# Issuing each 64 KB-row load of a decode attention kernel as two interleaved half transfers, one on SP's queue and one on ACT's

## The chip, the core and the metric

One core of one Trainium2 chip runs the whole program. The metric is device time in microseconds (us) of one execution, as the median of several runs. A profiled execution gives, besides its own time, a trace of every instruction and of every DMA queue.

## What is computed

A decode step (one token for each of two batch rows) of a transformer block with adaptive layer norm. Cut to what matters:

```python
mod = (silu(c) @ w_mod).reshape(2, 6, 1, 512)          # sa, ca, ga, sb, cb, gb
h = layernorm(x) * (1 + ca) + sa
q = (h @ wq) as 32 heads of 128
p = softmax(q . k_cache / sqrt(128))                   # 2 batches, 32 heads, 4096 keys
x = x + ga * ((p @ v_cache) @ wo)
h = layernorm(x) * (1 + cb) + sb
x = x + gb * (mish(h @ w1 + b1) @ w2)
```

All of it is float32. The two caches are 2 x 32 x 4096 x 128 each, so the work on one head begins with 4 MB of keys and 4 MB of values that are read once and never again. The weights come on top: 297 MB are read in all.

## The kernel before

**The stream.** Everything large comes from HBM as a stream of 36 loads, numbered 0 to 35, laid out beforehand in `stream` (line 31) so that a load is one array with 128 rows, one for each SBUF partition. Load 0 is two transfers with rows of 32 KB: the first holds the weights m01 (shift and scale of the first norm), wq0 and wq1, the second the keys k0 of head 0. Loads 1 to 31 are one transfer each, with rows of 64 KB (`ROW` = 16384 floats, 8 MB in all; sizes here are in units of 1024): the keys of head n and, in what room is left, halves of values, a wq or a wo. Loads 32 to 35 are twelve smaller transfers: one with rows of 56 KB for load 32, two of 32 KB for load 33, three for load 34 and six for load 35.

**The rooms.** `load` (line 134) takes one of three buffers, "room", of 64 KB per partition in turn and issues the load's transfers by `nc.sync.dma_start` (line 141), that is, on the queue of SP. `used` (line 146) keeps account: when every key of load n-3 has been used, load n is issued into the same room. It is called once at the start, which issues loads 0, 1 and 2 at once (line 156), and then after each step that finishes with a part of a room. No scheduler moves anything: the instructions of each engine stand in the order in which the Python code issues them, and each waits by semaphores for what it needs.

**The start.** On ACT's queue the kernel issues two small transfers: `cx` (line 161: 8 rows of 1 KB, the conditioning vector c and the token x) and `bias` (line 164: 128 rows of 48 bytes). From `cx` come the silu of c (`cps`, `sg`, `ct`) and the first layer norm (`mean_a`, `var_a`, `rs_a`, `xn`). With m01 in room 0, `modulation` (line 240) gives `modps`; from it come `hq`, `hps`, `hcw` (lines 270 to 280), and `project_q` (line 286) multiplies by wq0 and wq1; ACT scales the product into `q0` and `q1` (line 292).

**One head.** VectorE (DVE) does the scores: `products` (line 318) multiplies the keys in the room by q, in place, and `sums` (line 321) adds up over the 128 elements. `row_max` (lines 326 to 330) and `soft_max` (line 334 on DVE, line 337 on ACT) give the exponentials `e`, TensorE multiplies them by the values in `weighted_v` (line 359), and every four heads `value_sums`, `head_values` and `project_o` (lines 374, 382, 385, 390) bring the result through wo. The loop over the 32 heads issues `products(h)`, `soft_max(h-1)`, any `project_q`, `sums(h)`, then `used(("k", h))` (line 446), then the values whose load has come with these keys, then `row_max(h)`. So load h+3 is as a rule issued behind `sums(h)` in the code, or a little later, behind the last matmul on the values of that room.

**The end.** After head 31 come the rest of the values, the second norm, the two dense layers (`w1ps` line 514, `yps` line 556) and the store of 32 rows (line 566).

Of the kernel before, what the change touches and what calls it, by code (L numbers as in the profile page):

```python
# [13 lines left out]
P = 128  # L14
# [13 lines left out]
ROW = 2 * BIG  # L28
# [41 lines left out]
def kernel(  # L70
# [15 lines left out]
    nc = tc.nc  # L86
# [29 lines left out]
    def take(t, keys):  # L116
        lo = 0
        for key in keys:
            kind, n = key[:2]
            part = t[:, lo : lo + SIZES[kind]]  # L120
            lo += SIZES[kind]
            if kind == "k":
                k_t[n] = part.rearrange("p (j d) -> p j d", d=DH)
            elif kind == "v":
                v_t[n, key[2]] = part.rearrange("p (c n) -> p c n", n=512)
            elif kind in ("wq", "wo"):
                (wq_t if kind == "wq" else wo_t)[n] = part.rearrange("p (k n) -> p k n", k=G)
            else:
                w_t[kind] = part.rearrange("p (k n) -> p k n", k=NCH if kind == "w2" else G)
# [4 lines left out]
    def load(n):  # L134

        t = kvp.tile([P, ROW], F32, tag="room", name=f"room{n}", bufs=3)
        lo = 0
        for keys, srcs in loads[n]:
            take(t[:, lo:], keys)
            for src in srcs:  # L140
                nc.sync.dma_start(out=t[:, lo : lo + src.shape[-1]], in_=src)  # L141
                lo += src.shape[-1]

    loaded = 0
# [1 line left out]
    def used(*keys):  # L146

        nonlocal loaded
        done.update(keys)
        while loaded < len(loads) and (  # L150
            loaded < 3 or all(key in done for keys, _ in loads[loaded - 3] for key in keys)
        ):
            load(loaded)
            loaded += 1
# [16 lines left out]
        out=fold, in_=ident.rearrange("p (g r) -> p r g", g=G), axis=AX.X, op=ALU.add  # L171
# [3 lines left out]
        out=mean_w, in0=fold[:, None, :].to_broadcast([P, G, R]), scalar1=1.0 / D, scalar2=None, op0=ALU.mult  # L175
# [4 lines left out]
        out=half, in_=ident.rearrange("p (b r) -> p r b", b=B), axis=AX.X, op=ALU.add  # L180
# [330 lines left out]
    for k in range(G):  # L511
        lo = 0
# [9 lines left out]
    lo = 0  # L522
    for g in reversed(range(G)):
# [3 lines left out]
        lo = hi  # L527
# [112 lines left out]
```

## Time and profile before

| | us |
|---|---|
| median of 3 runs | 698.69 (698.48 to 698.77) |
| the profiled execution, its own time | 698.42 |
| its span, first to last instruction | 696.6 |
| DVE busy in the span | 587.7 (84%) |
| PE (matmul) busy | 283.8 (41%) |
| ACT busy | 44.0 (6%) |

The page of the profile gives the span in 40 slices of 17.4 us, with the busy share of each engine in tenths, the mean busy share of the 16 DMA engines and the GB/s that they moved. The queue of SP appears in the DMA list as q1, that of ACT as q10. "L318 DVE" is an instruction of line 318 on DVE. The view of DMA issues gives for each line the size and the median time from issue to landing. The chain of waits goes back from the last instruction to what released it.

### The profile page before, as it was taken

How to read it: one execution, taken by the hardware profiler on the slowest of the kernel's cores; microseconds unless marked ns; L12 is line 12 of the kernel's file. 1: busy time of each engine (PE TensorE's matmuls, PEld its weight loads, DVE VectorE, ACT ScalarE, POOL GpSimd, SP SyncE). 2: the span in 40 equal slices, each digit the busy share in tenths (PEclk: the TensorE clock that was granted, in tenths of full speed). 3: DMA queues.
4: the chain of work that ended last, by engine and by line, in shares of the span. 5: the costliest groups of instructions: out<-in, count | busy, mean ns of one | idle time of the engine just before them, and what ended most of it. 6: DMA issues, size and time to landing. Idle time of an engine off the chain costs nothing.

```text
span 696.6 us, 3912 instructions
## 1 busy us (share of the span) xinstructions
PE 283.8 (41%) x1636; PEld 102.4 (15%) x1636; DVE 587.7 (84%) x220; ACT 44.0 (6%) x168; POOL 4.2 (1%) x19
## 2 busy tenths in 40 slices
PE   3403334335245615335232806234333526224686
PEld 1200001001011201102100301011101101001234
DVE  3799899999999999999999999999999999899002
ACT  1000000000000000000000000000000000000010
POOL 2000000000000000000000000000000000000000
PEclk9855666667566665656585756666575657555789
DMA  9999999999999999999999999999999999999996
GB/s 392 452 421 421 426 474 421 419 429 421 467 422 425 429 425 456 429 425 426 433 448 429 426 429 437 440 430 429 433 437 437 429 425 422 452 427 420 423 422 270
DMA packets 6706, 297.49 MB, mean 427 GB/s; under 512 B 888, under 2 KB 928, under 8 KB 1184
## 3 DMA queue, kind: packets, MB, share of 16 engines
q1 hardware_dynamic: 6528, 297.23, 98.9%
q8 instruction: 13, 0.21, 0.1%
q10 hardware_dynamic: 160, 0.01, 0.0%
q14 instruction: 5, 0.04, 0.0%
HBM read 297.22 MB, written 0.02 MB: 427 GB/s over the span
## 4 chain that ended last, share of the span: by engine, by line
DMA 69%; DVE 28%; PE 2%; issue 0%; SPq 0%; ACT 0%; DVEq 0%
DMA room<-in_load 69%; DVE room L318 14%; DVE s L321 14%; PE ov L359 1%; PE qps L291 1%; PE modps L247 1%; PE yps L556 0%; SPq L141 0%; DVE m L334 0%; DVE hcw L280 0%; ACT q L292 0%; PE hps L237 0%; DVE y L564 0%; DVE hq L270 0%; DVE hq L271 0%
## 5 line engine op out<-in xcount | busy, mean ns | idle before, releaser
L318 DVE TENSOR_TENSOR room<-room,q 128x8192 f32<-128x8192 f32 x32 | 278.2, 8692 | 46.8 <-DMA room<-in_load 42.4
L321 DVE TENSOR_REDUCE s<-room 128x64 f32<-128x8192 f32 x32 | 277.9, 8683 | 0.4 <-DVE m L334 0.3
L359 PE MATMUL ov<-room,e 128*32 128x512 f32 x1024 | 176.4, 842 | 80.1 <-ACT e L337 63.9
L330 PE MATMUL mt<-d,same 128*128 128x64 f32 x64 | 18.2, 378 | 195.8 <-DVE d L328 195.8
L359 PEld LDWEIGHTS ov<-room,e 128*32 128x32 f32 x1024 | 39.2, 145 | 188.6 <-issue 133.8
L337 ACT ACTIVATE e<-s,m 64x64 f32<-64x64 f32 x64 | 22.1, 345 | 556.6 <-DVE m L334 555.8
L330 PEld LDWEIGHTS mt<-d,same 128*128 128x128 f32 x64 | 13.1, 254 | 225.8 <-DVE d L328 179.3
L291 PE MATMUL qps<-room,hcw 128*128 128x512 f32 x64 | 43.4, 844 | 4.8 <-DMA room<-in_load 4.0
L345 PE MATMUL l<-l,ones 128*128 128x8 f32 x16 | 4.6, 358 | 75.1 <-ACT e L337 75.1
L382 PE MATMUL otp<-pick,o 128*128 128x8 f32 (+2 forms) x72 | 13.4, 313 | 33.9 <-ACT o L374 32.0
L291 PEld LDWEIGHTS qps<-room,hcw 128*128 128x128 f32 x64 | 16.8, 274 | 26.4 <-issue 20.5
L374 DVE COPY o<-ov 128x256 f32<-128x256 f32 x1 | 0.4, 425 | 22.6 <-ACT o L374 22.6
L382 PEld LDWEIGHTS otp<-pick,o 128*128 128x128 f32 x72 | 12.6, 263 | 42.3 <-ACT o L374 39.4
L345 PEld LDWEIGHTS l<-l,ones 128*128 128x128 f32 x16 | 3.8, 296 | 76.5 <-ACT e L337 76.5
L334 DVE TENSOR_REDUCE m<-mt 128x1 f32<-128x64 f32 x32 | 6.9, 217 | 7.6 <-PE mt L330 7.6
L390 PE MATMUL att<-room,ot 128*32 128x512 f32 x62 | 10.1, 709 | 5.2 <-DMA room<-in_load 4.7
L337 ACT ACTIVATION_READ_ACCUMULATOR e<-s,m 64x1 f32 x64 | 11.8, 185 | 0.0
L328 DVE TENSOR_SCALAR d<-half,m 128x64 f32<-128x64 f32 x32 | 8.1, 254 | 1.1
L247 PE MATMUL modps<-room,ct 128*32 128x128 f32 (+1 forms) x160 | 8.1, 346 | 2.3 <-DMA room<-in_load 2.2
L326 DVE TENSOR_REDUCE m<-s 128x1 f32<-128x64 f32 x32 | 7.0, 217 | 0.9
L374 ACT COPY o<-ov 128x512 f32<-128x512 f32 (+1 forms) x9 | 5.0, 561 | 25.9 <-PE ov L359 25.7
L247 PEld LDWEIGHTS modps<-room,ct 128*32 128x32 f32 x160 | 5.0, 121 | 4.6 <-issue 4.4
(101 smaller groups left out, 60.6 us busy)
## 6 DMA issues: line engine op xcount, KB each, us to landing
room<-in_load SPq DMA_DIRECT2D x4, 4096.0 KB, 25.0
room<-in_load SPq DMA_DIRECT2D x1, 7168.0 KB, 39.1
room<-in_load SPq DMA_DIRECT2D x1, 3072.0 KB, 26.2
room<-in_load SPq DMA_DIRECT2D x3, 1024.0 KB, 28.3
room<-in_load SPq DMA_DIRECT2D x1, 2400.0 KB
room<-in_load SPq DMA_DIRECT2D x1, 2304.0 KB, 20.4
room<-in_load SPq DMA_DIRECT2D x1, 1376.0 KB, 15.8
room<-in_load SPq DMA_DIRECT2D x2, 256.0 KB, 22.8
```

The lines of the kernel that those rows point to most:

```text
L247: nc.tensor.matmul(ps[R * g : R * (g + 1)], lhsT=ct[:, k, :], rhs=t[:, k, :].rearrange("p (m n) -> p m n", m=n)[:, :, P * g : P * (g + 1)] ...
L291: nc.tensor.matmul(ps, lhsT=hcw[:, k, :], rhs=wq_t[ch][:, k, :], start=(k == 0), stop=(k == G - 1))
L318: nc.vector.tensor_tensor(out=k_t[h], in0=k_t[h], in1=qv, op=ALU.mult)
L321: nc.vector.tensor_reduce(out=s_t[h], in_=k_t[h], axis=AX.X, op=ALU.add)
L326: nc.vector.tensor_reduce(out=m_t[h][:, 0:1], in_=s_t[h], axis=AX.X, op=ALU.max)
L328: nc.vector.tensor_scalar(out=d, in0=half, scalar1=m_t[h][:, 0:1], scalar2=None, op0=ALU.mult)
L330: nc.tensor.matmul(mps[h], lhsT=same, rhs=d, start=True, stop=True)
L337: nc.scalar.activation(e_t[i][own_b, :, M * i + 4 * b : M * i + 4 * b + 4], s_t[h][own_b].rearrange("p (c m) -> p c m", m=4), AF.Exp, bias ...
L345: nc.tensor.matmul(lps[n], lhsT=ones, rhs=sum_t[n % 2], start=True, stop=True)
L359: nc.tensor.matmul(ov[bank][R * g : R * (g + 1), :], lhsT=e_t[h % HC][:, NB // 2 * part + c, :], rhs=v_t[h, part][:, c, :], start=(first a ...
L382: nc.tensor.matmul(tps[:, x], lhsT=o_t[m], rhs=pick_t[n][:, m, x], start=(m == 0), stop=(m == 3),)
L390: nc.tensor.matmul(att[R * i : R * (i + 1), :], lhsT=ot_t[n % 2][:, i, :], rhs=wo_t[n][:, i, :], start=(n == 0), stop=(n == H // HC - (2 i ...
```

## The change

The inner loop of `load` issues a transfer with rows of 64 KB as two: the rows of the even partitions by SP and those of the odd partitions by ACT, each 64 rows of 64 KB. All the other transfers stay one transfer on SP.

```diff
             for src in srcs:
-                nc.sync.dma_start(out=t[:, lo : lo + src.shape[-1]], in_=src)
+                queues = (nc.sync, nc.scalar) if src.shape[-1] == ROW else (nc.sync,)
+                for i, queue in enumerate(queues):
+                    rows = slice(i, P, len(queues))
+                    queue.dma_start(out=t[rows, lo : lo + src.shape[-1]], in_=src[rows])
                 lo += src.shape[-1]
```

It meets loads 1 to 31. In the program that comes of it SP has as many transfers as before, 31 of them with 64 rows in place of 128; ACT has 31 more. The odd halves of loads 1 and 2 stand first on ACT, ahead of `cx`, since line 156 comes before line 161. From load 3 on, ACT's half stands where `used` issues it: behind the exponentials of head n-4 and ahead of those of head n-3, and it waits for the same things as SP's half (the DVE and PE instructions that last read the room, and the transfers that last wrote it). Three lines are added, so line 318 of before is line 321 after, and so on.

## The prediction

> **What bounds the kernel now.** I read the page first: busy shares, then the DMA lines, then the chain that ended last.
>
> ```profile
> span 696.6 us, 3912 instructions
> PE 283.8 (41%) x1636; PEld 102.4 (15%) x1636; DVE 587.7 (84%) x220; ACT 44.0 (6%) x168; POOL 4.2 (1%) x19
> ...
> q1 hardware_dynamic: 6528, 297.23, 98.9%
> ...
> q10 hardware_dynamic: 160, 0.01, 0.0%
> ...
> DMA 69%; DVE 28%; PE 2%; issue 0%; SPq 0%; ACT 0%; DVEq 0%
> ```
>
> The packets of SP's queue (q1) fill 98.9% of the time of 16 engines. The chain's 28% on DVE looks like a second bound, so I looked at stretches of 100 us (the last two columns are DMA share and GB/s) and at DVE in order of time.
>
> ```profile
> 200.00:300.00 100.00, 44.69 (x208) 14.79 (x204) 93.11 (x28) 6.49 (x25) 0.00 (x0) 0.65 1.00 433
> 300.00:400.00 100.00, 39.70 (x192) 13.74 (x184) 93.06 (x28) 5.73 (x23) 0.00 (x0) 0.67 1.01 435
> 400.00:500.00 100.00, 32.00 (x158) 12.04 (x158) 93.08 (x30) 7.20 (x28) 0.00 (x0) 0.63 1.00 431
> ```
>
> ```profile
> 61.36 8.69 DVE L318 TENSOR_TENSOR room<-room,q 128x8192 f32<-128x8192 f32 x1 [1.39 <-DMA room<-in_load]
> ...
> 79.13 0.26 DVE L328 TENSOR_SCALAR d<-half,m 128x64 f32<-128x64 f32 x1
> 82.01 8.69 DVE L318 TENSOR_TENSOR room<-room,q 128x8192 f32<-128x8192 f32 x1 [2.63 <-DMA room<-in_load]
> ```
>
> DVE is done with a head 18.1 us after it began (61.36 to 79.4) and then waits for the next load. The chain in order of time gives the pace of the loads:
>
> ```profile
> 0.73 12.16 DMA room<-in_load
> ...
> 22.94 8.70 DVE room L318
> 31.64 0.02 issue
> 31.66 8.70 DVE s L321
> 40.36 0.02 SPq L141
> 40.38 0.04 issue
> 40.42 41.49 DMA room<-in_load
> ...
> 99.56 40.52 DMA room<-in_load
> 140.08 0.03 issue
> ```
>
> A room is issued again when `sums` of its head ends (40.36), and what was issued lands some 40.5 us later, two load times, because two other loads are ahead of it. Three loads land between 40.42 + 41.49 = 81.9 and 140.08, in 58.2 us: **19.4 us a load**, against 18.1 us on DVE. The DMA engines never run dry (share 1.00) and are the bound. For later: a load has 128 rows, 8 for each of 16 engines, so a 64 KB row holds an engine for 19.4 / 8 = 2.42 us, a 32 KB row for 1.21 us. The first transfer (4 MB, 9.7 us) lands at 12.89, so starting from a dry queue costs 12.89 - 9.7 - 0.73 = 2.46 us from issue to landing beyond the moving itself.
>
> **The change, steady part.** The bytes and the number of rows stay. Each load has two transfers in place of one, 31 more in all. A shorter time has no idle time to come from: the share is 1.00. How fast 64 rows of every second partition move beside the other 64 no row shows. Bounds: at the best stretch's 435 instead of 433 GB/s, 31 x 19.4 x 0.5% = 3 us less; if two engines at a time hinder each other altogether, every row takes 4.85 us, 31 x 19.4 = 601 us more. I take the row nearest to it, the same 64 KB rows from HBM to SBUF on q1: **no change**. One completion packet more for each engine and load I take at nothing too (cover: none; bound from `bias` below, where eleven small turns fit with no time of their own).
>
> On ACT come 31 issues, at the 0.36 us of its own issue below some 11 us on an engine that is busy 44.0 of 696.6 us. Its new wait holds up, until `sums` ends, what stands behind: the exponentials of that head, which need `m` of L334, one 8.69 us product later anyway, and in some heads the copy L374 with `otp` on PE behind it, which has the same 8.69 us of cover before DVE needs `mt`. DVE now waits for two transfers; the extra semaphore instruction is 21 ns in before (x8), under 1 us for 31, in DVE's slack of 19.4 - 18.1.
>
> ```profile
> L318 DVEq EVENT_SEMAPHORE  x8: 21/21/21, 22.7 to 566.4; - x8
> ```
>
> ```profile
> 2.26 0.36 ACTq L164 DMA_DIRECT2D bias<-in_b1c  x1
> ```
>
> **The change, start.** Here something moves. The odd halves of loads 1 and 2 are issued on ACT ahead of `cx` and `bias`.
>
> ```profile
> bias<-in_b1c ACTq DMA_DIRECT2D x1, 6.0 KB, 15.5
> ```
>
> ```profile
> 8.09 0.57 PE L237 MATMUL cps<-ident,cx 128*128 128x8 f32 x2 [8.09 <-DMA cx<-in_head]
> ...
> 9.45 0.17 DVE L261 TENSOR_TENSOR ct<-cps,sg 128x8 f32<-128x8 f32 x1
> ...
> 12.86 0.34 DVE L266 TENSOR_SCALAR xn<-xc_a,rs_a 128x128 f32<-128x128 f32 x1
> ...
> 13.03 3.64 PE L247 MATMUL modps<-room,ct 128*32 128x256 f32 x32 [1.21 <-DMA room<-in_load]
> ...
> 16.73 0.29 DVE L270 SCALAR_TENSOR_TENSOR hq<-modps,xn 128x128 f32<-128x128 f32 x1 [3.52 <-PE modps L247]
> ...
> 22.31 0.60 ACT L292 ACTIVATE q<-qps 128x512 f32<-128x512 f32 x1 [9.96 <-PE qps L291]
> ```
>
> `bias` is 6 KB and takes 15.5 us to land. That tells how an engine divides itself between q1 and q10: `cx`, its completion, eight bias rows and their completion are 11 turns, and 11 x 1.21 + 2.46 = 15.8. So the two queues take **turns, packet by packet**, whatever a packet's size.
>
> [...]
>
> With turns, the first transfer on SP (8 rows of 32 KB an engine, one completion) meets ACT's 4 + 4 rows of 64 KB and two completions, and `cx` with its completion comes after 3 more rows of k0. By the landing of before (3.2 us plus the moving): `cx` lands at 3.2 + 11 x 1.21 + 8 x 2.42 = **35.9** in place of 8.09; k0 at 3.2 + 16 x 1.21 + 19.4 = 42.0. From `cx` on nothing is faster: `xn` and `modps` 5.2 us after `cx` (8.09 to 13.2; 9.6 + 3.7 likewise), `hq` to the first product 22.94 - 16.73 = 6.2. The first product starts at 35.9 + 5.2 + 6.2 = **47.3** (k0 is there) instead of 22.94, and `sums` of head 0 ends 17.4 later at 64.7.
>
> That delay of 24 us is hidden as far as loads 1 and 2 last. The bytes of loads 0 to 2 are the same, so all have landed near 61.36. Load 3 is issued at 64.7 into a dry queue and lands at 64.7 + 2.46 + 19.4 = 86.6. Without a hole it lands at 61.36 + 19.4 = 80.8; in before it came at 82.0, and what the 1.2 us are I can't place. So the hole is 4.6 to 5.8 us, and I take 5.2. It is the only one: load 4 is issued 18.1 us after load 3, before that one has landed, and DVE gains 1.3 us on each load until it waits again as before (after some 24 / 1.3 = 18 heads). The end is untouched.
>
> **Sum:** 698.42 + 0 + 5.2 = 703.6 us. The profiled execution stands 0.27 us under the median of the runs shown, and 1.8 us over its span, which I leave as they are.
>
> **Rivals.**
>
> 1. *Engines in each other's way.* That 16 engines move 433 GB/s together is shown only with 8 of 128 rows for each. With 64 rows each has 4, and which partitions these are no row shows. If pairs of engines then write to one place that lets through only one engine's pace, and all start together at an issue, a row takes up to 4.85 us and a load 38.8. DVE (18.1) hides nothing of that. Each of 31 loads costs 19.4 more: 698.4 + 601 = 1299 (the start lies inside). If they meet half the time: about 1000. A pair that gets ahead runs dry and starts together again at the next issue, so the full price is likelier than the half. Against: no packet of before shows such a pace. [...]
> 2. *Turns by bytes.* If an engine gave both queues equal bytes, `cx` would land after 3.2 + 2 x 19.4 = 42 plus a row, 43.2: 7.3 us later, 711. The 15.5 of `bias` speak against it.
> 3. *ACT's rows in one burst: not slower.* If ten or more packets of ACT pass in a row, `cx` lands at 3.2 + 19.4 = 22.6 and m01 at 32.3; `modps`, `hq` to product: 42.3; `sums` ends at 59.7, before loads 1 and 2 have run out; load 3 lands at 81.6 against 80.8 to 82.0, no hole, 698.6. It decides as soon as the first product starts before some 42.8. The 15.5 of `bias` speak against it.
> 4. *A faster pace*, the 3 us of the bound. Alone it leaves 700.6; only with rival 3 is it faster than before, 695.6.
>
> **Chances.** Forecast 0.42; rival 1 in full 0.30, in part (anything from 720 to 1200) 0.15; rival 2 0.05; rival 3 0.05; rival 4 with 3, 0.03. Likeliest is 703.6, its own range 700 to 709. The range that holds 8 in 10 must take in rival 1: 700 to 1305; outside lie rival 3, rival 4 with 3 and a little beyond the doubling. About 0.2% (1.4 us) is what a measurement can tell from no change: faster 0.03, same 0.05, slower 0.92.
>
> **What would show it.** Right: the first L321 starts near 47 (L318 of before), waiting for ACT's q; DMA share well under 1 in a few us after 61, then 1.00; products 18.1 us apart up to about head 18, then 19.4. Rival 1: DMA share 1.00 at about 216 GB/s, products 38.8 us apart, DVE under half busy. Rival 2 or 3: first product near 55 or 42. Wrong, too, if `cx` were not late at all, or if a later hole appears where ACT issues its half after SP's.

## The result and the profile after

The change makes the kernel **slower: 711.26 us against 698.66, ratio 1.0178 (95% interval 1.0165 to 1.019)**, 12.6 us. The profiled execution took 709.83 us (span 708.0), 11.4 us more than the one of before; it is the quickest of four, which reach from 709.83 to 711.81. The four executions of before beside it lie between 698.48 and 698.77, its profiled one took 698.42.

The page of the changed kernel, first the DMA share in 40 slices with the GB/s, then the two queues:

```profile
DMA  9994999999999999999999999999999999999996
GB/s 385 434 426 178 415 464 422 418 460 419 426 444 430 429 437 434 422 437 434 426 433 444 426 434 437 423 438 441 422 437 441 423 429 444 427 428 422 425 420 272
...
q1 hardware_dynamic: 4544, 167.20, 55.0%
q10 hardware_dynamic: 2640, 130.04, 42.5%
```

The even rows are on q1, the odd ones on q10, together 97.5% of the engines' time in place of 98.9%. There is one hole, in the fourth slice, and from there on the rate is that of before. The windows of the same kernel show both (the last three columns are granted TensorE clock, DMA share and GB/s):

```profile
62.00:70.00 8.00, 0.00 (x0) 0.00 (x0) 7.96 (x2) 0.00 (x0) 0.00 (x0) 0.50 0.00 0
...
300.00:400.00 100.00, 41.01 (x188) 14.68 (x188) 93.03 (x28) 6.48 (x25) 0.00 (x0) 0.61 1.00 431
400.00:500.00 100.00, 39.33 (x182) 14.77 (x182) 92.06 (x30) 6.33 (x24) 0.00 (x0) 0.67 1.00 434
```

From 62 to 70 us not one packet moves. How the hole comes about stands in the chain of waits up to the first issue after it (start, duration, what):

```profile
1.96 35.09 DMA cx<-in_head
37.05 0.14 issue
37.18 0.58 PE cps L240 x2
...
38.96 0.60 PE mean_a L213 x2
...
40.35 0.56 PE var_a L221 x2
40.91 3.55 PE modps L250 x32
...
44.48 0.30 DVE hq L273
...
45.15 0.40 PE hps L240 x2
...
46.32 5.41 PE qps L294 x8
51.73 0.02 issue
51.75 0.61 ACT q L295
52.36 0.02 issue
52.38 8.70 DVE room L321
61.08 0.02 issue
61.11 8.70 DVE s L324
```

`cx`, 8 KB, is on its way for 35 us, and the first product starts at 52.38 in place of 22.94. Load 3 is issued only when this head's sums end:

```profile
69.82 0.52 ACTq L144 DMA_DIRECT2D room<-in_load  x1
```

By the packets in the trace (start and end of each row that an engine moves), the last rows of loads 0 to 2 end at 61.1 us and the first of load 3 begin at 71.1.

Much later the loads come at the old pace, and DVE waits a little for each again:

```profile
306.71 8.69 DVE L321 TENSOR_TENSOR room<-room,q 128x8192 f32<-128x8192 f32 x1 [1.42 <-DMA room<-in_load]
326.00 8.69 DVE L321 TENSOR_TENSOR room<-room,q 128x8192 f32<-128x8192 f32 x1 [1.27 <-DMA room<-in_load]
345.47 8.69 DVE L321 TENSOR_TENSOR room<-room,q 128x8192 f32<-128x8192 f32 x1 [1.44 <-DMA room<-in_load]
```

19.4 us apart, as before. The last product starts at 637.1 us, in before at 625.6: the 11.5 us are lost at the start and stay as they are to the end.

### The profile page after: what moved, and what is told of

Read it like the earlier page. It is cut to its first block, busy times and chain, and to the rows that moved or that the text cites. A ratio compares the mean times of both kernels' runs of the same rounds, so it can differ in the third digit from the quotient of the medians.

```text
span 708.0 us, 4080 instructions
## 1 busy us (share of the span) xinstructions
PE 285.3 (40%) x1636; PEld 104.2 (15%) x1636; DVE 586.6 (83%) x220; ACT 44.0 (6%) x168; POOL 4.2 (1%) x19
## 2 busy tenths in 40 slices
DMA packets 7202, 297.50 MB, mean 420 GB/s; under 512 B 1384, under 2 KB 1424, under 8 KB 1680
## 4 chain that ended last, share of the span: by engine, by line
DMA 48%; DVE 43%; issue 5%; PE 3%; ACT 0%; SPq 0%; POOL 0%; DVEq 0%; ACTq 0%; POOLq 0%
DMA room<-in_load 43%; DVE room L321 23%; DVE s L324 19%; DMA cx<-in_head 5%; PE ov L362 1%; PE qps L294 1%; PE modps L250 1%; DVE m L329 0%; PE yps L559 0%; SPq L144 0%; ACT e L340 0%; DVE m L337 0%; ACT q L295 0%; DVE hcw L283 0%; PE mean_a L213 0%
## 5 line engine op out<-in xcount | busy, mean ns | idle before, releaser
L240 PE MATMUL cps<-ident,cx 128*128 128x8 f32 x2 | 0.6, 358 | 37.2 <-DMA cx<-in_head 37.2
## 6 DMA issues: line engine op xcount, KB each, us to landing
room<-in_load SPq DMA_DIRECT2D x1, 7168.0 KB, 38.8
```

## The experiments

**Theory:** the whole loss is the late `cx`, and the split itself costs nothing. **Rival:** each split load costs something, 11.4 / 31 = 0.37 us. The first four kernels tell these apart.

### The two small transfers first

```diff
-    used()
     cx = const.tile([P, 2, P], F32, name="cx")
     ...
     nc.scalar.dma_start(out=bias, in_=b1c)
+    used()
```

> All of the change, but the two small transfers cx and bias are issued on ACT ahead of the odd halves of loads 1 and 2. Theory (the start: cx late behind 8 MB on ACT's queue, nothing else): cx is back near 8 us, m01 near 13; k0 shares turns with the odd rows and lands near 42, the first product starts there, sums of head 0 end near 59.5, load 3 is issued just before loads 0 to 2 have run out near 61, so hardly a hole: 698.7 to 699.5. Rival (the split costs something on every load, 11.4 / 31 = 0.37 us each): 710.

698.69 us, ratio 1.0001 (0.9992 to 1.001). All 31 loads are split, and nothing is lost. The rival falls. Its timeline on PE and DVE:

```profile
8.21 0.57 PE L238 MATMUL cps<-ident,cx 128*128 128x8 f32 x2 [8.21 <-DMA cx<-in_head]
...
34.95 8.69 DVE L319 TENSOR_TENSOR room<-room,q 128x8192 f32<-128x8192 f32 x1 [16.07 <-DMA room<-in_load]
```

Now the first product waits for k0 and not for q. It starts at 34.95 where 42 was expected: `cx` and `bias` take the first eleven turns of ACT's queue beside m01's rows and the first rows of k0, so that, by the packets in the trace, four 64 KB rows an engine fall between the rows of k0 and not eight. That the first product is 12 us later than in before costs nothing.

### Only loads 3 to 31 split, and only loads 1 and 2

```diff
-queues = (nc.sync, nc.scalar) if src.shape[-1] == ROW else (nc.sync,)
+queues = (nc.sync, nc.scalar) if src.shape[-1] == ROW and n > 2 else (nc.sync,)   # the one
+queues = (nc.sync, nc.scalar) if src.shape[-1] == ROW and n < 3 else (nc.sync,)   # the other
```

> Only loads 3 to 31 are split, loads 1 and 2 stay whole on SP. Theory (the start): the start is that of before, 698.7, within 0.2%. Rival (a cost on every split load): 29 x 0.37 = 10.7 more, 709.4.

698.92 us, ratio 1.0003 (0.9994 to 1.0012).

> Only loads 1 and 2 are split, loads 3 to 31 are whole on SP. Theory (the start): the whole loss, 709.8 to 711.8. Rival (a cost on every split load): 2 x 0.37, 699.4.

711.3 us, ratio 1.0179 (1.0163 to 1.0194), single executions from 709.41 to 712.78. Two split loads cost all of it, 29 nothing. Its chain is that of the changed kernel, with other numbers:

```profile
38.48 0.56 PE L240 MATMUL cps<-ident,cx 128*128 128x8 f32 x2 [38.48 <-DMA cx<-in_head]
...
55.31 8.69 DVE L321 TENSOR_TENSOR room<-room,q 128x8192 f32<-128x8192 f32 x1 [7.47 <-ACT q L295]
```

The first product is 2.93 us later than in the changed kernel's profile, and the profiled execution (712.78) 2.95 us longer.

### A late `cx` with nothing split

```diff
-    used()
     cx = const.tile([P, 2, P], F32, name="cx")
     nc.gpsimd.memset(cx, 0.0)
-    nc.scalar.dma_start(out=cx[::TB], in_=head)
+    load(0)
+    load(1)
+    nc.sync.dma_start(out=cx[::TB], in_=head)
+    load(2)
+    loaded = 3
```

> The kernel of before with nothing split; cx alone is late, issued on SP behind load 1 and ahead of load 2. Theory (the start): cx lands near 42 with m01 and k0 on time, the first product starts 14 to 15 us later near 57, sums of head 0 end near 74, load 3 lands near 96 instead of 81.5: 713, some 14 us more, and executions spread by a microsecond or two, as the exposed TensorE chain is throttled now and then. Rival (the split itself, or m01 and k0 delayed by the turns): nothing is split and both are on time, 698.7.

715.19 us, ratio 1.0237 (1.0221 to 1.0253); expected were 713. The late `cx` alone does it, with m01 and k0 on time (by the packets their last rows end at 12.7 and 22.4 us, in before at 12.5 and 22.2):

```profile
42.49 0.57 PE L238 MATMUL cps<-ident,cx 128*128 128x8 f32 x2 [42.49 <-DMA cx<-in_head]
...
57.91 8.69 DVE L319 TENSOR_TENSOR room<-room,q 128x8192 f32<-128x8192 f32 x1 [6.06 <-ACT q L293]
```

### Half the burden ahead of `cx`

```diff
+queues = (nc.sync, nc.scalar) if src.shape[-1] == ROW and n == 1 else (nc.sync,)
```

> Only load 1 is split; load 2 and all others are whole on SP. So cx stands on ACT behind 4 rows of 64 KB an engine in place of 8. Theory (the loss is what the first product starts after a point near 41 us, and nothing before it): cx lands near 3.2 + 7 x 1.21 + 4 x 2.42 = 21.4, the first product starts 15 to 17 us later near 37, before loads 1 and 2 have run out: no loss, 698.7 to 699.0, although the first product is 14 us later than before. Rival (the loss goes with the delay of the first product): half of it, 705.

698.73 us, ratio 1.0002 (0.9992 to 1.0012). `cx` is 15 us late and the first product too, and nothing is lost:

```profile
22.84 0.57 PE L240 MATMUL cps<-ident,cx 128*128 128x8 f32 x2 [22.84 <-DMA cx<-in_head]
...
38.41 8.69 DVE L321 TENSOR_TENSOR room<-room,q 128x8192 f32<-128x8192 f32 x1 [6.21 <-ACT q L295]
```

The profiled executions together:

| kernel | `cx` used at | first product | profiled time | time less first product |
|---|---|---|---|---|
| before | 8.09 | 22.94 | 698.42 | |
| loads 3 to 31 split | 8.27 | 24.34 | 698.83 | |
| `cx` first | 8.21 | 34.95 | 698.63 | |
| load 1 split | 22.84 | 38.41 | 698.79 | |
| the change | 37.18 | 52.38 | 709.83 | 657.45 |
| loads 1 and 2 split | 38.48 | 55.31 | 712.78 | 657.47 |
| late `cx`, no split | 42.49 | 57.91 | 715.20 | 657.29 |

In the last three rows, each microsecond by which the first product is later is a microsecond of the total; up to 38.41 us the delay is free. Carried back, the last column gives 698.6 - 657.4 = 41.2 us as the point where the loss begins. That point is an estimate: no kernel lies between 38.41 and 52.38.

### Other ways to cut a load

Rival 1 of the prediction, engines that hinder each other, did not show. Was the mechanism wrong, or do even and odd rows avoid it? Four kernels cut the same loads by other rows; the first has `cx` and `bias` ahead on ACT, the others leave ACT as in before.

```diff
+rows = slice(i * P // len(queues), (i + 1) * P // len(queues))   # halves, SP and ACT
+rows = slice(i * P // parts, (i + 1) * P // parts)   # halves, both on SP (parts = 2)
+rows = slice(i, P, parts)   # even and odd, both on SP (parts = 2)
+rows = slice(i, P, parts)   # every fourth, all four on SP (parts = 4)
```

> As in the run with cx and bias ahead on ACT, but SP takes partitions 0 to 63 and ACT 64 to 127 of each 64 KB-row load, in place of even and odd ones. Theory (an engine is held 2.42 us by a 64 KB row wherever it lands; rival 1 of the prediction is void for every split): 698.7 to 699.5. Rival (rival 1 holds for contiguous halves, the even and odd rows only happen to avoid it): DMA share near 1.00 at about 216 GB/s, products about 38.8 us apart, towards 1300.

1268.19 us, and far apart: four executions took 1234.98, 1252.34, 1284.03 and 1304.24. The theory of the expectation falls.

> The kernel of before, but each 64 KB-row load is two transfers on SP, partitions 0 to 63 and then 64 to 127; nothing is added to ACT. Theory (a row holds an engine 2.42 us wherever it lands, and a second transfer and its completions cost nothing): 698.7, within 0.2%. Rival (engines that fill one half of the partitions at a time get in each other's way): each half takes as long as a whole load did, products 38.8 us apart, towards 1300; in between if only part of the time.

1352.0 us, ratio 1.9346 (1.9303 to 1.939). So something like rival 1 exists. The products of the halves on one queue, and a window (DMA share and GB/s last):

```profile
307.99 8.69 DVE L321 TENSOR_TENSOR room<-room,q 128x8192 f32<-128x8192 f32 x1 [22.46 <-DMA room<-in_load]
348.52 8.69 DVE L321 TENSOR_TENSOR room<-room,q 128x8192 f32<-128x8192 f32 x1 [22.51 <-DMA room<-in_load]
```

```profile
300.00:400.00 100.00, 20.46 (x87) 6.13 (x87) 46.71 (x15) 3.80 (x14) 0.00 (x0) 0.60 1.02 210
```

A load takes 40.5 us, 2.09 times 19.4, while all engines count as busy: a share of 1.02 at 210 GB/s. By the packets in the trace a 64 KB row holds an engine for 5.13 us (median) in place of 2.42. The busy share alone would not have told.

> The kernel of before, but each 64 KB-row load is two transfers on SP, the even partitions and then the odd ones; it differs from the run with halves on one queue (1352) only in which rows a transfer has. Theory (what makes the halves slow is that one transfer reaches half of the partitions; even rows reach as much as all 128): 698.7, within 0.2%, rows 2.42 us. Rival (it is the second queue that keeps even and odd rows fast, by mixing both transfers): slow here too, 1000 to 1350.

698.85 us, ratio 1.0003 (0.9993 to 1.0013).

> As the run with even and odd rows on one queue, but four transfers of every fourth partition, 32 rows each, two for each of 16 engines. At most eight transfers are under way at once, two loads. Theory (an engine's rows are dealt so that each engine keeps to a part of the partitions of its own, whatever the step): 698.7 to 700. Rival (each engine takes neighbouring rows of the transfer, and with 64 rows it was luck): two or more engines meet, 1000 to 1350.

700.0 us, ratio 1.002 (1.0011 to 1.0029). The pace is the full one in both; first even and odd, then every fourth:

```profile
300.00:400.00 100.00, 41.61 (x177) 14.56 (x176) 93.12 (x28) 5.73 (x23) 0.00 (x0) 0.62 1.01 435
```

```profile
300.00:400.00 100.00, 41.22 (x180) 14.71 (x176) 93.08 (x28) 5.73 (x23) 0.00 (x0) 0.64 1.01 434
```

Halves and even/odd on one queue differ in nothing but the rows of each transfer, 1352 against 699. Not the second queue keeps even and odd rows fast, but which rows a transfer has. The same slice cuts the rows in HBM and the partitions in SBUF, so these runs do not tell whether the halves are slow where they are read or where they are written. Where the 1.4 us of every fourth come from is open.

The price of the halves is about the one that rival 1 put on 64 rows at a time: a 64 KB row takes 5.13 us, where rival 1 had up to 4.85, and the rate is 210 GB/s, where before had 433. Even and odd rows have 64 rows in a transfer too and every fourth 32, and both run at the full pace (435 and 434 GB/s), so it isn't the number of rows. The last two expectations gave theories of which partitions a transfer or an engine reaches; the times came out as those theories had them, 698.85 and 700.0, but no view shows how the rows are dealt to the engines or what a contiguous half does to them.

## Why the prediction was wrong, point by point

**Right:** the bound, the pace of 19.4 us a load, the split at no cost (loads 3 to 31 split: 698.92), the turns packet by packet, the single hole, load 4 in time, and direction. The packets in the trace show the turns: while m01 shares them with 64 KB rows, an engine's 32 KB rows begin 3.6 to 3.8 us apart, one row of 1.21 and one of 2.42. `bias` took 48.5 us in place of 15.5, one 48-byte row between two large ones.

**Wrong: the size of the hole.** It was forecast as 5.2 us; the loss is 12.6 in the medians and 11.4 between the profiled executions. The step that failed is "From `cx` on nothing is faster: ... 5.2 us after `cx`, `hq` to the first product 6.2": the path from `cx` to the first product was put at 11.4 us and measured 52.38 - 37.18 = 15.2. Term by term:

- `cx` itself: 37.18 instead of 35.9, 1.3 us, about one 32 KB row (1.21). With only loads 1 and 2 split, where the start is the same code, it came another 1.3 us later: by the packets, three 32 KB rows of an engine go ahead of ACT's first row there, two in the changed kernel.
- `cx` to `hq`: 7.3 instead of 5.2 us. I let `modps` start when `ct` was ready, as if PE were free. On PE the matmuls `mean_a` and `var_a` stand ahead of `modps`, and `var_a` needs a chain over DVE; `modps` started 3.7 us after `cx`, right behind `var_a`. In before that order was hidden by m01 (13.03, "<-DMA room").
- `hq` to the first product: 7.9 instead of 6.2. The eight matmuls of `qps` took 5.41 us in place of the 3.71 of before:

```profile
18.57 3.71 PE qps L291 x8
```

  That 3.71 is the shortest of the seven traces of the table. In the others these matmuls took 5.1 to 6.8 us up to `q`, in the kernels that lost nothing too.
- The landing that load 3 would have had: I took the middle of 80.8 and 82.0. Issued at 69.85 it lands by my rule at 69.85 + 2.46 + 19.4 = 91.7 (by the packets its last rows end at 91.5), which is 10.9 after the 80.8. The 1.2 us that I couldn't place come in the changed kernel too, one load later: the rows of load 3 end 10.0 us later than in before, those of load 4 11.2. So the lower end was the right one, 0.6 us.

That is 1.3 + 2.1 + 1.7 + 0.6 = 5.7 of the 6.2 us missing between the profiled executions; 0.5 stay open.

A smaller miss: DVE waited for a load again at head 13, at 287.27 us, not at about head 18. I let it make up the whole delay of 24 us, but the hole itself gives part of that back: when load 3 lands at 91.7, head 3 is 14.4 us away (106.05), and with products 17.9 us apart DVE gains 1.4 to 1.5 us a load, so ten loads.

**Why the median is 1.4 us above the profiled execution.** The eight `qps` matmuls vary from trace to trace. Their group in the changed kernel (min/median/max in ns) and the granted clock while they run:

```profile
L294 PE MATMUL qps<-room,hcw x16: 592/592/1061, 46.3 to 54.6; 128*128 128x512 f32 x16
```

```profile
47.50:51.00 3.50, 3.50 (x5) 1.35 (x4) 0.00 (x0) 0.00 (x0) 0.00 (x0) 0.52 0.82 356
```

The granted clock stood at 0.52 from 47.5 to 51 (the third number from the end). Up to `q` the `qps` matmuls took 3.71 us in before, 5.41 here, 6.8 with only loads 1 and 2 split (47.89 to 54.68). In before this lies beside the loads and costs nothing; past some 41 us it adds to the total, and so does the 1.3 us by which `cx` varies. That fits the spread of single executions (2.0, 3.4 and 1.5 us in four each where the start is exposed, 0.8 in 19 of before) and the 1-to-1 of the table. For the executions without a trace it is argued, not shown. What lowers the clock no view shows. The 0.52 stands behind a stretch with the clock at 1.00 in which matmuls fill 1.57 of 3 us (44.5 to 47.5). Two matmuls of one shape took 0.58 us at 37.18, behind 37 us without a matmul, and 0.40 at 45.15, though the granted clock stands at 1.00 for both. With only loads 1 and 2 split the record of the granted clock doesn't show a slow stretch: it stands at 1.00 from 50 to 52, where three matmuls fill 2 us, and the longest of the group takes 1222 ns.

```profile
L294 PE MATMUL qps<-room,hcw x16: 592/604/1222, 47.9 to 57.5; 128*128 128x512 f32 x16
```

```profile
50.00:52.00 2.00, 2.00 (x3) 0.77 (x3) 0.00 (x0) 0.00 (x0) 0.00 (x0) 1.00 1.22 525
```

The late `cx` has a longest of 1222 ns too, with the clock at 1.00 from 20 to 60 us, so the throttling that its expectation names is not shown there:

```profile
20.00:60.00 40.00, 13.96 (x55) 6.99 (x56) 5.57 (x15) 1.24 (x4) 0.00 (x0) 1.00 1.00 434
```

**The rivals.** Rival 2's 711 was hit by chance: `cx` came by turns, at 37.2, not by bytes at 43.2. Rival 3 (a burst) fell with it. Rival 1 had 0.45 of the chance and stretched the range to 1305. Its price is real for halves (40.5 us a load against the 38.8 forecast); for even and odd rows it doesn't arise. Before a run nothing in the trace of before could have told the two apart.

## What to carry to other kernels

A transfer's cost can lie in what stands behind it: two halves of 4 MB ahead of an 8 KB transfer on the same queue held up the whole start (`cx` used at 37.18 us in place of 8.09, 711.26 us in all), and moving the two small transfers ahead took the loss away (698.69). When a hidden start becomes the critical path, walk it again in the order of each engine's queue and give each duration the spread of several traces, since what was hidden was never measured as a limit: the one trace of before had the shortest `qps` of all (3.71 us against 5.1 to 6.8). If a load must be cut by partitions, interleaving them cost nothing here (698.85 us on one queue), and contiguous halves nearly a factor of two (1352.0), at a full busy share (1.02).

## What the runs showed that I had not expected

- Contiguous halves of 64 partitions ran at 201 to 210 GB/s on one queue and 220 to 221 on two (from 200 to 400 us), against 431 to 435 for all rows, even/odd rows or every fourth row.
- On two queues the halves got faster in the course of the profiled execution. In one window early and one late:

```profile
100.00:200.00 100.00, 18.45 (x102) 5.16 (x102) 53.81 (x15) 2.62 (x12) 0.00 (x0) 0.59 0.97 210
...
900.00:1000.00 100.00, 24.62 (x114) 9.46 (x114) 54.03 (x17) 3.44 (x15) 0.00 (x0) 0.59 1.01 269
```

  By the packets the time of a 64 KB row falls with it, from 4.84 us (median, 100 to 200) to 3.78 (900 to 1000). Why is not shown.
- One more completion packet for each engine and load (4 bytes; the trace of before has 16 for each of SP's 46 transfers) cost nothing that could be measured: even and odd rows on one queue moved 7202 packets against 6706, 31 x 16 more, in 698.85 us.
